# 512-token input products for six more state blocks of an S5 scan kernel, and layernorm deviations and means for four chunks at once

## The chip, the cores and the metric

One NeuronCore of a Trainium2 chip. The metric is the device time of one execution in microseconds (us); the kernel before takes 250.15 us, median of 3 runs (250.13 to 250.19).

## The reference

Input A_x is 2048 tokens by 1024 columns in bf16. It is normalised per token (xn), and the output is x plus two branches of xn, cut here to what matters:

```python
xn = layernorm(x)
# branch A: a diagonal complex state space with P = 1024 states
Bu = einsum("bld,pd->blp", xn, B_bar)           # input products, complex
h[t] = Lam_bar * h[t-1] + Bu[t]                 # scan over 2048 tokens
y  = 2 * real(einsum("blp,dp->bld", h, C)) + xn * Dskip
# branch B: the two tokens with the largest xn @ w_r go through a gated MLP (F = 3584)
out = x + y + xn + scatter(mlp(xn[top2]))
```

## The kernel before, in words

**Tiles.** Tokens come in 16 chunks of 128 (c), 8 frames of 256 (f) and 4 super-frames of 512 (s). States come in 8 blocks of 128 (j), each with a real and an imaginary part (ri).

**Order of the work.** The body registers small tasks with a planner (`add`), each with an engine, a function and its dependencies. The long string `ORDER` lists all tasks in one fixed sequence, and `emit` issues them in it. So each engine's own queue is the subsequence of its tasks, and an engine that reaches a task whose input is not there waits, with all that stands behind it. A ring (`pl.ring`) bounds how many buffers a kind of tile has; the products' PSUM tiles `pB` have 3.

**A chunk's normalisation.** Chunks 0 to 5 get their mean and variance on VectorE (`bs.c`, `bn.c`, lines 312 to 320), the others on ScalarE (`sum.c`, `sq.c`). `rstd.c` (line 336, `inv_sqrt` at 281) is three ScalarE instructions on one column: logarithm `lv`, reciprocal deviation, and deviation (line 286). `nmr1.c` adds 1 to the deviation (GpSimd line 360, ScalarE line 369) and `mean.c` negates the negated mean (GpSimd line 363). `apply.c` writes the normalised chunk. For chunks 0 to 3 TensorE transposes it (`Tpe.c`, line 386) and `xnT.c` copies it out of PSUM (VectorE for chunk 0, ScalarE line 393 for the rest); later chunks are transposed by DMA (`T.c`).

**The start on TensorE.** 15 warming tasks (`warm`), the transposes of the first blocks of B (`tB.0`, `tB.1`, line 262; ScalarE copies them out as `B.0.0`, `B.0.1`), of the parameters (`pP`, line 474; VectorE `pcol`), and of the chunks. The transposed blocks `B.j.ri` for j over 0 come by DMA from SyncE's queue.

**Input products.** For the first two super-frames (s below `SFW = 2`) a task `Bu.f.j` (line 661) makes both parts of one block for a frame: 16 matmuls over 256 tokens, into one PSUM bank, which ScalarE copies out in one instruction (`u.f.j`, line 667). For f below 2 and j below 2 each is split in halves of 128 tokens (`Bh.f.j.ri`, then `Bu`). For the last two super-frames a task `Bs.s.j.ri` (line 672) makes one part for 512 tokens: 8 matmuls over 512 tokens, also one bank, and ScalarE copies it out in two instructions of 256 (`us.s.j.ri`, line 680).

**Scan and output.** Per frame VectorE turns the products (`TI.f`, lines 738 to 747), scans per chunk (`SC.c`, line 766); ScalarE casts (`gb.c`, line 772); GpSimd carries the state on (`cw.c` 782, `cy.c` 790, `cin.c` 797 and 798); VectorE turns back (`TO.c`, lines 808 to 817). Per chunk and column half (dh) ScalarE seeds a PSUM tile with xn (`seed.c.dh`, line 871), VectorE applies the skip row and the deviation (`sk.c.dh`, line 881), TensorE adds 16 matmuls of 512 columns (`Y.c.0` to `Y.c.3`, eight each, line 891; 0 and 1 are the left half, 2 and 3 the right), ScalarE adds the mean (`ADD.c.dh`, line 907), SyncE stores. These PSUM tiles are a ring of 3: `seed.2.0` takes the buffer that `ADD.0.1` gives back, which reads the end of `Y.0.3`.

Of the kernel before, what the change touches and what calls it, by code (L numbers as in the profile page):

```python
# [25 lines left out]
warm.0 warm.1 warm.2 warm.3 warm.4 warm.5 warm.6 Bn.0 x.0 xa bs.0 bn.0 rstd.0 pre x.1 bs.1 apply.0 bn.1 warm.7 warm.8 warm.9 warm.10 warm.11 warm.12  # L26
warm.13 warm.14 tB.0 start.0 nmean.1 x.2 B.1.0 x.3 Tpe.0 Bn.1 B.1.1 B.0.0 xnT.0 bs.2 rstd.1 apply.1 tB.1 Bh.0.0.0 Tpe.1 x.5 bn.2 bs.3 B.0.1 nmean.0
xnT.1 bn.3 rstd.2 B.2.0 Bh.0.0.1 pP.0 pcol.0 Bh.0.1.0 apply.2 rstd.3 dt frq x.4 B.3.0 B.2.1 Bu.0.0 u.0.0 Bh.0.1.1 Tpe.2 rad Bu.0.1 apply.3 xnT.2 Tpe.3
turns xnT.3 B.3.1 Bh.1.0.0 Bh.1.0.1 Bh.1.1.0 Bu.1.0 trig bs.5 B.4.0 u.0.1 whole angle bn.5 nmean.5 abs u.1.0 sin den bs.4 first Bh.1.1.1 Bu.1.1 u.1.1
cos Bu.0.2 B.4.1 sq1.0 u.0.2 Bu.1.2 Bu.0.3 nmean.2 sq1.1 bn.4 log inv.0 rc.0 u.1.2 rstd.5 kappa mean.0 Bu.1.3 Bu.1.4 nmean.3 nmr.1 R0.0 apply.5 B.5.0  # L30
B.5.1 x.6 tan.0 inv.1 u.0.3 rc.1 tan.1 cs ntan.0 Bu.0.4 u.1.3 rstd.4 u.1.4 Bu.1.5 TI.0.0 ntan.1 u.0.4 ts.1.1 ends cin.0.0 nmr.5 ts.1.0 nmean.4 nmr1.2
nmr.0 apply.4 u.1.5 B.6.0 B.6.1 ts.0.0 Bu.0.5 Bu.0.6 u.0.5 T.5 sum.6 nmean.6 Bu.1.6 B.7.0 B.7.1 Bu.0.7 nmr1.1 T.4 x.7 nmr.4 R0.1 R.1 ts.0.1 u.0.6 sq.6
rstd.6 nmr1.6 nmr.6 apply.6 u.1.6 Bu.1.7 R.0 SC.0.0.0 xr.0 xnT.4 SC.0.0.1 C.0.1 sum.7 E2c.1 nmean.7 xnT.5 u.0.7 u.1.7 x.8 T.6 E2c.0 Bu.2.0 Bu.2.1
Bu.2.2 x.9 gb.0.0.0 sq.7 u.2.0 nmr1.3 cw.0.0 nmr1.0 seed.0.0 TI.0.4 E2s.0 wr cy.0.0 cin.1.0 rstd.7 gb.0.0.1 nmr.7 u.2.1 Bu.2.3 xnT.6 Bu.2.4 nmr.2
cin.0.4 SC.0.4.0 cw.0.4 SC.0.4.1 cy.0.4 apply.7 u.2.2 sum.8 Drow T.7 gb.0.4.0 u.2.3 xr.1 u.2.4 gb.0.4.1 E2n.0 xnT.7 SC.1.0.0 cw.1.0 cin.1.4 SC.1.0.1
E2s.1 SC.1.4.0 Bu.2.5 Bu.2.6 Bu.2.7 u.2.5 nmean.8 E2n.1 SC.1.4.1 nmr1.4 u.2.6 sq.8 nmr.3 TO.0.4 C.0.0 sk.0.0 seed.0.1 sk.0.1 u.2.7 seed.1.0 sum.9
nmean.9 Bu.3.0 u.3.0 gb.1.0.0 rstd.8 gb.1.4.0 sq.9 TO.0.0 nmr.8 mean.2 gb.1.4.1 Bu.3.1 u.3.1 apply.8 gb.1.0.1 Bu.3.2 u.3.2 Bu.3.3 rstd.9 Y.0.0 Y.0.1
C.1.0 TI.1.0 u.3.3 ADD.0.0 nmr.9 apply.9 cw.1.4 cy.1.4 cin.2.4 cy.1.0 Bu.3.4 Bu.3.5 x.11 Bu.3.6 T.8 Y.0.2 TO.1.4 cin.2.0 SC.2.0.0 sk.1.0 x.10 E2t.1
TO.1.0 u.3.4 seed.1.1 sum.10 nmean.10 sq.10 C.1.1 cw.2.0 gb.2.0.0 SC.2.0.1 cy.2.0 cin.3.0 T.9 xr.2 x.12 Y.1.0 Y.0.3 sk.1.1 rstd.10 mean.1 E2t.0
gb.2.0.1 Y.1.1 Bu.3.7 SC.3.0.0 sum.11 nmean.11 sq.11 nmr.10 ADD.0.1 apply.10 seed.2.0 rstd.11 TO.2.0 ADD.1.0 nmr.11 u.3.5 Y.1.2 Y.1.3 seed.2.1 ADD.1.1  # L40
out.0.1 apply.11 sk.2.0 T.10 x.15 out.0.0 SC.3.0.1 cw.3.0 sk.2.1 Y.2.0 gb.3.0.0 Y.2.1 Y.2.2 xnT.9 u.3.6 TI.2.0 xr.3 gb.3.0.1 u.3.7 T.11 sum.15 sum.12
ADD.2.0 Y.2.3 mean.10 cy.3.0 cin.4.0 SC.4.0.0 cw.4.0 xnT.11 nmean.15 xnT.8 xnT.10 sq.15 TO.3.0 SC.4.0.1 cy.4.0 mean.3 mean.7 nmean.12 seed.3.0 sk.3.0
rstd.15 Bs.2.0.0 us.2.0.0 Bs.2.0.1 cin.5.0 out.2.0 Bs.2.1.0 Bs.2.1.1 seed.3.1 us.2.0.1 ADD.2.1 gb.4.0.0 us.2.1.0 gb.4.0.1 Bs.2.2.0 TO.4.0 SC.5.0.0
SC.5.0.1 Y.3.0 xr.5 xr.4 us.2.1.1 x.13 seed.4.0 x.14 sq.12 nmr.15 rstd.12 apply.15 us.2.2.0 nmr.12 apply.12 out.1.1 T.15 sk.3.1 Bs.2.2.1 Bs.2.3.0
us.2.2.1 us.2.3.0 Bs.2.3.1 Bs.2.4.0 Y.3.1 Y.3.2 gb.5.0.0 out.1.0 mean.5 mean.12 cw.5.0 gb.5.0.1 cy.5.0 cin.6.0 nmr1.5 nmr1.10 sum.13 nmean.13 us.2.3.1
TI.3.0 SC.6.0.0 T.12 mean.4 SC.6.0.1 cw.6.0 cy.6.0 mean.11 us.2.4.0 Bs.2.4.1 cin.7.0 sq.13 ADD.3.0 rstd.13 xnT.12 seed.4.1 us.2.4.1 sum.14 nmean.14
sq.14 nmr.13 sk.4.0 sk.4.1 rstd.14 nmr.14 Y.3.3 Bs.2.5.0 gb.6.0.0 us.2.5.0 apply.14 Bs.2.5.1 Bs.2.6.0 Y.4.0 Y.4.1 Bs.2.6.1 out.2.1 gb.6.0.1 T.14
apply.13 T.13 xnT.15 xnT.13 ADD.3.1 nmr1.9 us.2.5.1 TO.5.0 xnT.14 SC.7.0.0 Y.4.2 ADD.4.0 us.2.6.0 seed.5.0 us.2.6.1 TO.6.0 Y.4.3 r.0 seed.5.1 out.4.0
out.3.0 gb.7.0.0 Bs.2.7.0 Bs.2.7.1 sk.5.0 w.0 SC.7.0.1 cand ADD.4.1 sk.5.1 us.2.7.0 us.2.7.1 w.1 xr.6 out.3.1 w.2 w.3 TI.4.0 Y.5.0 Y.5.1 ADD.5.0
gb.7.0.1 idx cw.7.0 cy.7.0 cin.8.0 seed.6.0 gather SC.8.0.0 SC.8.0.1 Bs.3.0.0 Bs.3.0.1 seed.6.1 us.3.0.0 Y.5.2 us.3.0.1 sk.6.0 bns gb.8.0.1 nmr1.13  # L50
cw.8.0 cy.8.0 xz Bs.3.1.0 us.3.1.0 Bs.3.1.1 Bs.3.2.0 us.3.1.1 us.3.2.0 Y.5.3 ADD.5.1 rstds Y.6.0 Bs.3.2.1 gb.8.0.0 us.3.2.1 out.5.0 w.4 sig TO.7.0
norm Bs.3.3.0 w.5 cin.9.0 sT out.5.1 xT SC.9.0.0 gb.9.0.0 nmr1.15 Y.6.1 mm.0 SC.9.0.1 sk.6.1 cw.9.0 nmr1.8 nmr1.7 mean.6 cy.9.0 TI.5.0 xr.7 Bs.3.3.1
gb.9.0.1 us.3.3.0 us.3.3.1 seed.7.0 sk.7.0 out.4.1 cin.10.0 Bs.3.4.0 Y.6.2 Y.6.3 mean.13 w.6 sig1 TO.8.0 ADD.6.0 w.7 w.8 w.9 Y.7.0 w.10 w.11 ADD.6.1
seed.7.1 sk.7.1 SC.10.0.0 xr.8 Bs.3.4.1 Bs.3.5.0 mm.1 Y.7.1 Y.7.2 SC.10.0.1 cw.10.0 ymb0 us.3.4.0 cy.10.0 us.3.4.1 seed.8.0 xr.9 exp.0 ADD.7.0
gb.10.0.0 out.6.0 TO.9.0 out.6.1 Bs.3.5.1 gu.0 gb.10.0.1 sk.8.0 Y.7.3 us.3.5.0 seed.8.1 ADD.7.1 Bs.3.6.0 us.3.5.1 us.3.6.0 Bs.3.6.1 mean.8 cin.11.0
SC.11.0.0 SC.11.0.1 cw.11.0 cy.11.0 cin.12.0 mean.9 w.12 Bs.3.7.0 w.13 w.14 w.15 w.16 w.17 out.7.0 out.7.1 xr.10 gb.11.0.1 seed.9.0 gb.11.0.0 nmr1.11
Bs.3.7.1 us.3.6.1 us.3.7.0 us.3.7.1 sk.8.1 gT.0 mm.2 exp.1 TO.10.0 sk.9.0 Y.8.0 Y.8.1 Y.8.2 Y.8.3 ADD.8.0 w.18 w.19 w.20 w.21 w.22 w.23 w.24 w.25
out.8.0 seed.9.1 ADD.8.1 TI.6.0 SC.12.0.0 SC.12.0.1 Y.9.0 cw.12.0 seed.10.0 sk.9.1 TO.11.0 sk.10.0 Y.9.1 Y.9.2 gb.12.0.1 ADD.9.0 xr.11 out.9.0 out.8.1
seed.10.1 mm.3 Y.9.3 xr.12 gb.12.0.0 cy.12.0 cin.13.0 SC.13.0.0 nmr1.12 sk.10.1 Y.10.0 gu.1 Y.10.1 Y.10.2 Y.10.3 cw.13.0 mean.14 gb.13.0.0 ADD.9.1
TO.12.0 w.26 w.27 w.28 seed.11.0 exp.2 ADD.10.0 seed.11.1 gT.1 mm.4 sk.11.0 ADD.10.1 sk.11.1 SC.13.0.1 w.29 w.30 out.9.1 w.31 w.32 w.33 w.34 w.35  # L60
out.10.0 xr.13 out.10.1 seed.12.0 sk.12.0 gu.2 TI.7.0 gT.2 Y.11.0 Y.11.1 ADD.11.0 seed.12.1 Y.12.0 Y.12.1 Y.11.2 Y.11.3 xr.14 gb.13.0.1 TO.13.0
sk.12.1 cy.13.0 ADD.11.1 ADD.12.0 exp.3 cin.14.0 SC.14.0.0 cw.14.0 seed.13.0 seed.13.1 sk.13.0 SC.14.0.1 mm.5 Y.12.2 Y.12.3 cy.14.0 cin.15.0 out.11.1
gb.14.0.0 gu.3 sk.13.1 ADD.12.1 gb.14.0.1 Y.13.0 Y.13.1 Y.13.2 Y.13.3 out.11.0 w.36 w.37 w.38 out.12.0 TO.14.0 w.39 nmr1.14 seed.14.0 ADD.13.0
ADD.13.1 sk.14.0 SC.15.0.0 hot w.40 seed.14.1 out.13.0 w.41 out.12.1 gT.3 xr.15 Y.14.0 Y.14.1 SC.15.4.0 SC.15.0.1 sk.14.1 SC.15.4.1 mm.6 Y.14.2
ADD.14.0 seed.15.0 seed.15.1 SC.15.6.0 rows Y.14.3 ADD.14.1 seed.15.2 TO.15.0 sk.15.1 sk.15.0 TO.15.4 row_.3 out.13.1 row_.2 out.14.0 SC.15.6.1
# [1133 lines left out]
```

## Time and profile before

| | |
|---|---|
| median of 3 runs | 250.15 us (250.13 to 250.19) |
| the profiled execution | 250.2 us, of it 248.1 us in the profile's span and 2.1 us around it |
| TensorE | 241.1 us busy |
| VectorE / ScalarE / GpSimd | 231.0 / 177.4 / 92.1 us busy |
| TensorE's granted clock | 0.998 of full |

The profile lists instructions by engine: PE is TensorE, PEld its weight loads, DVE VectorE, ACT ScalarE, POOL GpSimd, SPq SyncE's DMA issues. The chain of waits follows the execution back from its last instruction: each piece is what released the next. A group "x48" is that many instructions of one line. Matmuls overlap in their pipeline, so the length of one in a list is more than the step from one to the next; steps are read from groups.

### The profile page before, as it was taken

How to read it: one execution, taken by the hardware profiler on the slowest of the kernel's cores; microseconds unless marked ns; L12 is line 12 of the kernel's file. 1: busy time of each engine (PE TensorE's matmuls, PEld its weight loads, DVE VectorE, ACT ScalarE, POOL GpSimd, SP SyncE). 2: the span in 40 equal slices, each digit the busy share in tenths (PEclk: the TensorE clock that was granted, in tenths of full speed). 3: DMA queues.
4: the chain of work that ended last, by engine and by line, in shares of the span. 5: the costliest groups of instructions: out<-in, count | busy, mean ns of one | idle time of the engine just before them, and what ended most of it. 6: DMA issues, size and time to landing. Idle time of an engine off the chain costs nothing.

```text
span 248.1 us, 4602 instructions
## 1 busy us (share of the span) xinstructions
PE 241.1 (97%) x1723; PEld 139.9 (56%) x1743; DVE 231.0 (93%) x267; ACT 177.4 (71%) x364; POOL 92.1 (37%) x148
## 2 busy tenths in 40 slices
...
GB/s 206 237 190 150 210 171 249 144 274 131 237 144 109 106 97 114 127 3 10 118 184 248 165 0 116 393 225 320 274 176 400 251 376 340 281 202 391 66 64 44
DMA packets 66753, 46.77 MB, mean 189 GB/s; under 512 B 46114, under 2 KB 52648, under 8 KB 66732
## 3 DMA queue, kind: packets, MB, share of 16 engines
...
q8 instruction: 13, 0.21, 0.3%
q10 hardware_dynamic: 192, 0.07, 0.1%
q14 instruction: 8, 0.07, 0.1%
...
## 4 chain that ended last, share of the span: by engine, by line
PE 94%; DMA 2%; issue 1%; DVE 1%; SPq 1%
PE pY L891 44%; PE pB L661 23%; PE pB L672 22%; PE pG L1086 3%; DMA xt<-in_A_x_dram 2%; PE pD L1117 1%; PE r_ps L404 1%; DVE ot L905 1%; PE pT L386 1%; SPq L180 0%; SPq L168 0%; DVE xn L346 0%; SPq L169 0%; PE pY L896 0%; PE pP L474 0%
## 5 line engine op out<-in xcount | busy, mean ns | idle before, releaser
L891 PE MATMUL pY<-CT,hT 128*128 128x512 bf16 (+1 forms) x515 | 113.1, 372 | 0.9 <-issue 0.3
L891 PEld LDWEIGHTS <-hT 128*128 128x128 bf16 x528 | 51.2, 98 | 58.9 <-issue 1.9
L766 DVE TENSOR_TENSOR_SCAN gf<-R,v 128x1040 f32<-128x1040 f32 (+1 forms) x34 | 68.9, 2055 | 1.4 <-POOL v L798 1.0
L782 POOL TENSOR_TENSOR cw<-gf,tL 128x16 f32<-128x16 f32 (+1 forms) x34 | 33.4, 984 | 97.5 <-DVE gf L766 89.8
L672 PE MATMUL pB<-xnT,BT 128*128 128x512 bf16 x249 | 57.0, 379 | 0.4
L661 PE MATMUL pB<-xnT,BT 128*128 128x256 bf16 (+1 forms) x576 | 57.3, 261 | 0.0
L661 PEld LDWEIGHTS <-BT 128*128 128x128 bf16 x576 | 51.1, 98 | 5.6
L907 ACT ACTIVATE ot<-pY,mean_all 128x512 bf16<-128x512 f32 x30 | 20.5, 686 | 33.4 <-PE pY L891 33.2
L672 PEld LDWEIGHTS <-BT 128*128 128x128 bf16 x256 | 24.8, 98 | 30.4 <-PE pG L1086 0.4
L772 ACT CAST gb<-gf 128x1024 bf16<-128x1024 f32 (+1 forms) x34 | 31.8, 940 | 7.5 <-DVE gf L766 7.3
L808 DVE TENSOR_TENSOR m<-gb,E 128x4096 bf16<-128x4096 bf16 x13 | 29.5, 2271 | 0.5 <-ACT gb L772 0.5
L680 ACT CAST u<-pB 128x256 bf16<-128x256 f32 x64 | 19.9, 376 | 10.0 <-PE pB L672 8.0
L871 ACT ACTIVATE pY<-xr,nmr_all,rstd_all 128x512 f32<-128x512 bf16 (+1 forms) x33 | 25.2, 770 | 0.3
L881 DVE SCALAR_TENSOR_TENSOR pY<-Drow,std_all,pY 128x512 f32<-128x512 bf16 (+1 forms) x33 | 23.5, 723 | 0.6 <-ACT pY L871 0.6
L667 ACT CAST u<-pB 128x512 bf16<-128x512 f32 x32 | 18.2, 578 | 2.1 <-PE pB L661 2.0
L810 DVE TENSOR_TENSOR hT<-m 128x2048 bf16<-128x2048 bf16 x13 | 15.9, 1225 | 1.2
L740 DVE TENSOR_TENSOR v<-u,m 128x4096 bf16<-128x4096 bf16 x7 | 16.0, 2292 | 0.2
L738 DVE TENSOR_TENSOR m<-u,E1t 128x4096 bf16<-128x4096 bf16 x7 | 16.0, 2283 | 0.0
L798 POOL TENSOR_TENSOR v<-cy,v 128x16 bf16<-128x16 f32 (+1 forms) x17 | 14.2, 837 | 1.4
L350 ACT ACTIVATE xn<-xt,nmr_all,rstd_all 128x1024 bf16<-128x1024 bf16 x10 | 12.4, 1238 | 0.1
L332 ACT ACTIVATE xn<-xt,nmean_all 128x1024 bf16<-128x1024 bf16 x10 | 11.5, 1153 | 0.1
L797 POOL CAST v<-cy 128x16 bf16<-128x16 f32 (+1 forms) x17 | 10.4, 610 | 0.8
...
## 6 DMA issues: line engine op xcount, KB each, us to landing
...
wt<-in_B_w_down_dram SPq DMA_DIRECT2D x4, 1024.0 KB, 10.7
...
```

Source lines behind the costliest of these rows:

```text
L661: nc.tensor.matmul(out=pB[:, ri, ts_], lhsT=BT[ri][j][:, k, :], rhs=xnT_frame(f)[:, k, ts_], start=(k == 0), stop=(k == DT - 1))
L667: nc.scalar.copy(out=u_tiles[f][:, :, :, j, :].rearrange("p c i t -> p i c t"), in_=pB_tiles.pop((f, j))[:].rearrange("p i (c t) -> p i c ...
L672: nc.tensor.matmul(out=pB[:], lhsT=BT[ri][j][:, k, :], rhs=xnT_tiles[s][:, k, :], start=(k == 0), stop=(k == DT - 1))
L680: nc.scalar.copy(out=u_tiles[f][:, :, ri, j, :], in_=pB[:, i * TF:(i + 1) * TF].rearrange("p (c t) -> p c t", c=CPF))
L766: nc.vector.tensor_tensor_scan(out=flat(gf), data0=flat(R[:, js, :]), data1=flat(v[:, ri, js, :]), initial=0.0, op0=ALU.mult, op1=ALU.add)
L772: nc.scalar.copy(out=gb_tiles[c][:, ri, js, :], in_=gf_tiles[c, js.start, ri][:, :, 2:])
L782: nc.gpsimd.tensor_tensor(out=cw_tiles[c, js.start][:, ri, :, 0:n], in0=g.unsqueeze(1).to_broadcast([128, 2, n]), in1=tL[:, ri, :, js], op ...
L808: nc.vector.tensor_tensor(out=m[:].rearrange("p k i j t -> p k (i j t)"), in1=E2[:].rearrange("p k i j t -> p k (i j t)"), in0=flat(gb[:]) ...
L871: nc.scalar.activation(out=pY[:, 0:d_.stop - d_.start], in_=y_tiles["xr", c][:, d_], func=ACT.Identity, bias=nmr_all[:, c:c + 1], scale=rs ...
L881: nc.vector.scalar_tensor_tensor(out=pY, in0=ms["Drow"][:, d_], scalar=std1_all[:, c:c + 1], in1=pY, op0=ALU.add, op1=ALU.mult)
L891: nc.tensor.matmul(out=pY, lhsT=h_tiles[c][:, ri, j, :], rhs=CT[ri][h][:, j, d0:d0 + w], start=False, stop=end, skip_group_check=True)
L907: nc.scalar.activation(out=ot, in_=pY, func=ACT.Identity, bias=mean_all[:, c:c + 1])
```

## The change

What it does, part by part.

1. `HY = (3, 7, 0, 0)` replaces `SFW`: in super-frame 0 the blocks 3 to 7, in super-frame 1 block 7, are made by `Bs` tasks of 512 tokens. That is six blocks; 192 matmuls of 256 tokens become 96 of 512, and 12 copies `u` become 24 narrower ones.
2. The logarithms of all chunks are kept (`lv_all`). `rstd.c` is two instructions. The deviations of four chunks are made by one instruction (`std.g`), the 1 is added for four by one GpSimd instruction (`nmr1.g`), and `mean.g` does four means. Each waits for all four chunks.
3. `ORDER` is written anew throughout.

```diff
-    SFW = 2
+    HY = (3, 7, 0, 0)
...
+    lv_all = consts.tile([128, NCH], F32, name="lv_all")
...
     def ln_rstd(c, scale):
-        inv_sqrt(rstd_all[:, c:c + 1], ln_part[c][:, 1:2], 128, scale, std1_all[:, c:c + 1])
+        nc.scalar.activation(out=lv_all[:, c:c + 1], in_=ln_part[c][:, 1:2], func=ACT.Ln, bias=eps_t[:], scale=scale)
+        nc.scalar.activation(out=rstd_all[:, c:c + 1], in_=lv_all[:, c:c + 1], func=ACT.Exp, scale=-0.5)
+
+    def ln_std(g):
+        nc.scalar.activation(out=std1_all[:, 4 * g:4 * g + 4], in_=lv_all[:, 4 * g:4 * g + 4], func=ACT.Exp, scale=0.5)
...
-    def ln_std1(c):
-        nc.gpsimd.tensor_scalar_add(out=std1_all[:, c:c + 1], in0=std1_all[:, c:c + 1], scalar1=1.0)
-
-    def ln_mean(c):
-        nc.gpsimd.tensor_scalar_mul(out=mean_all[:, c:c + 1], in0=nmean_all[:, c:c + 1], scalar1=-1.0)
+    def ln_std1(g):
+        nc.gpsimd.tensor_scalar_add(out=std1_all[:, 4 * g:4 * g + 4], in0=std1_all[:, 4 * g:4 * g + 4], scalar1=1.0)
+
+    def ln_mean(g):
+        nc.gpsimd.tensor_scalar_mul(out=mean_all[:, 4 * g:4 * g + 4], in0=nmean_all[:, 4 * g:4 * g + 4], scalar1=-1.0)
...
-    def ln_std1_act(c):
-        nc.scalar.activation(out=std1_all[:, c:c + 1], in_=std1_all[:, c:c + 1], func=ACT.Identity, bias=one_t[:])
...
+    for g in range(NSF):
+        four = range(4 * g, 4 * g + 4)
+        add(("std", g), "ACT", 0.2, lambda g=g: ln_std(g), [("rstd", c) for c in four] + [("log",)], key=4 * g - 24)
+        add(("nmr1", g), "POOL", 0.3, lambda g=g: ln_std1(g), [("std", g)], key=4 * g - 24)
+        add(("mean", g), "POOL", 0.3, lambda g=g: ln_mean(g), [("nmean", c) for c in four], key=4 * g - 24)
...
-    for s in range(SFW, NSF):
-        for j in range(PT):
+    for s in range(NSF):
+        for j in range(HY[s], PT):
             for ri in range(2):
...
-    for f in range(2 * SFW):
-        for j in range(PT):
+    for f in range(NF):
+        for j in range(HY[f // 2]):
```

The new `ORDER`, as the queues that it gives to the engines at the places that matter here ("..." is the same or without interest):

```
TensorE, start, before: warm x15  tB.0 Tpe.0 tB.1 Bh.0.0.0 Tpe.1 Bh.0.0.1 pP Bh.0.1.0 Bu.0.0 Bh.0.1.1 Tpe.2 Bu.0.1 Tpe.3
                        Bh.1.0.0 Bh.1.0.1 Bh.1.1.0 Bu.1.0 Bh.1.1.1 Bu.1.1 Bu.0.2 Bu.1.2 ...
TensorE, start, after:  warm x15  Tpe.0 tB.0 tB.1 pP Tpe.1 Bh.0.0.0 Bh.0.1.0 Bh.0.0.1 Tpe.2 Bu.0.0 Bh.1.0.0 Bh.1.0.1
                        Bh.1.1.0 Bh.0.1.1 Tpe.3 Bu.0.1 Bh.1.1.1 Bu.1.0 Bu.1.1 Bu.0.2 Bu.1.2 Bs.0.3.0 ... Bs.0.7.1 Bu.2.0 ...
VectorE, start, before: ... bs.2 apply.1 bn.2 bs.3 bn.3 pcol apply.2 frq apply.3 turns ...
VectorE, start, after:  ... bs.2 apply.1 bn.2 apply.2 pcol bs.3 frq bn.3 turns apply.3 ...
ScalarE, start, before: rstd.0 B.0.0 rstd.1 B.0.1 xnT.1 rstd.2 rstd.3 dt u.0.0 rad xnT.2 xnT.3 ...
ScalarE, start, after:  rstd.0 rstd.1 B.0.0 B.0.1 rstd.2 xnT.1 dt xnT.2 u.0.0 rstd.3 rad trig xnT.3 ...
TensorE, later, before: Bu.3.6 Y.0.2 Y.1.0 Y.0.3 Y.1.1 Bu.3.7 Y.1.2 Y.1.3 Y.2.0 Y.2.1 Y.2.2 Y.2.3 Bs.2.0.0 ...
TensorE, later, after:  Bu.3.6 Bs.1.7.0 Y.0.2 Bs.1.7.1 Y.1.0 Y.0.3 Y.1.1 Y.1.2 Y.2.0 Y.2.1 Y.2.2 Y.2.3 Y.1.3 Bs.2.0.0 ...
ScalarE, later, before: ... ADD.0.1 apply.10 seed.2.0 rstd.11 ADD.1.0 ...
ScalarE, later, after:  ... apply.10 sq.11 ADD.0.1 us.1.7.0 seed.2.0 ADD.1.0 sum.12 seed.2.1 us.1.7.1 ...
GpSimd, later, after:   ... cw.2.0 mean.0 nmr.3 mean.1 cy.2.0 ...
SyncE, start, before:   x.2 B.1.0 x.3 B.1.1 x.5 B.2.0 x.4 B.3.0 B.2.1 B.3.1 B.4.0 B.4.1 B.5.0 B.5.1 x.6 B.6.0 B.6.1 T.5 B.7.0 B.7.1 T.4 ...
SyncE, start, after:    x.2 B.1.0 x.3 B.1.1 x.4 B.2.0 B.2.1 B.3.0 x.5 B.4.0 B.3.1 B.5.0 B.4.1 x.6 B.5.1 T.4 B.6.0 B.6.1 B.7.0 B.7.1 x.7 T.5 ...
```

## Rows read from the trace of the kernel before

**Rows 1.** The page's first part: busy time, share of the span and instructions.
```profile
PE 241.1 (97%) x1723; PEld 139.9 (56%) x1743; DVE 231.0 (93%) x267; ACT 177.4 (71%) x364; POOL 92.1 (37%) x148
```

**Rows 2.** All waits of TensorE: who waited for whom, total us, times, longest.
```profile
PE warm L409 <- POOL ident masks.py:199: 1.4, 1, 1.4
PE pT L386 <- DVE xn L346: 0.9, 1, 0.9
PE pT L262 <- DMA Bn<-in_A_B_im_dram: 0.3, 1, 0.3
PE pY L891 <- issue: 0.3, 2, 0.2
```

**Rows 3.** Pieces of the chain that ended last: start us, us, what.
```profile
8.70 0.62 PE pT L386 x8
...
9.77 0.12 PE pP L474
...
12.37 0.89 PE pB L661 x16
13.26 0.45 PE pT L386 x8
13.71 45.49 PE pB L661 x448
...
62.65 5.24 PE pB L661 x48
...
76.55 0.65 PE pY L891 x3
...
138.95 5.18 PE pB L672 x24
...
243.96 1.57 DVE ot L905 x3
```

**Rows 4.** The timeline of the start: start us, us, engine, line, instruction, count.
```profile
7.14 0.61 PE L661 MATMUL pB<-xnT,BT 128*128 128x128 bf16 x8
...
9.28 0.21 DVE L320 BATCH_NORM_AGGREGATE mv<-st 128x2 f32<-128x12 f32 x1
...
10.27 0.30 ACT L283 ACTIVATE lv<-mv,eps_t 128x1 f32<-128x1 f32 x1
...
10.85 0.54 DVE L346 TENSOR_SCALAR xn<-xt,mv,rstd_all 128x1024 bf16<-128x1024 bf16 x1
...
12.40 1.01 ACT L393 COPY xnT<-pT 128x1024 bf16<-128x1024 bf16 x1 [0.19 <-PE pT L386]
```

**Rows 5.** Groups by line and shape: count, busy us, mean ns of one, idle before.
```profile
L661 PEld LDWEIGHTS <-BT 128*128 128x128 bf16 x576 | 51.1, 98 | 5.6
...
L680 ACT CAST u<-pB 128x256 bf16<-128x256 f32 x64 | 19.9, 376 | 10.0 <-PE pB L672 8.0 <-remote 2.0
L667 ACT CAST u<-pB 128x512 bf16<-128x512 f32 x32 | 18.2, 578 | 2.1 <-PE pB L661 2.0
...
L286 ACT ACTIVATE std_all<-lv 128x1 f32<-128x1 f32 x16 | 3.0, 186 | 0.0
...
L369 ACT ACTIVATE std_all<-std_all,one_t 128x1 f32<-128x1 f32 x10 | 2.7, 289 | 0.0
```

**Rows 6.** One 5 us window: busy us (count) by engine, TensorE's clock, DMA.
```profile
45.00:50.00 5.00, 5.00 (x49) 4.47 (x47) 4.80 (x8) 5.00 (x10) 4.76 (x8) 1.00 0.46 111
```

**Rows 7.** The timeline of SyncE's queue: the last transposing load of B.
```profile
28.92 1.48 SPq L240 DMA_TRANSPOSE BT<-in_A_B_im_dram  x1
```

**Rows 8.** The page's DMA issues: count, median us from issue to landing.
```profile
BT<-in_A_B_im_dram SPq DMA_TRANSPOSE x7, 4.1
```

**Rows 9.** The timeline before Y.2.0: the add of (0,1), the seed, the skip.
```profile
75.05 0.67 ACT L907 ACTIVATE ot<-pY,mean_all 128x512 bf16<-128x512 f32 x1
76.75 0.76 ACT L871 ACTIVATE pY<-xr,nmr_all,rstd_all 128x512 f32<-128x512 bf16 x1
...
77.55 0.75 DVE L881 SCALAR_TENSOR_TENSOR pY<-Drow,std_all,pY 128x512 f32<-128x512 bf16 x1
```

More of the change, by code (lines that the diff above doesn't have):

```diff
@@ L25 @@
 ORDER = """
[L26 to L65, printed above, removed]
@@ L66 @@
-sk.15.2 out.14.1 row_.1 ymb TO.15.6 Y.15.0 Y.15.1 Y.15.2 Y.15.3 Y.15.4 Y.15.5 Y.15.6 hotY.15.0 hotY.15.1 ADD.15.0 fix Y.15.7 hotY.15.2 out.15.0 Y.15.8
-ADD.15.1 out.15.1 ADD.15.2 out.15.2
+xa bs.0 x.0 bn.0 rstd.0 Bn.0 x.1 bs.1 apply.0 bn.1 pre warm.0 warm.1 warm.2 warm.3 warm.4 warm.5 start.0 Bn.1 x.2 rstd.1 B.1.0 warm.6 warm.7 warm.8
+warm.9 warm.10 warm.11 warm.12 x.3 warm.13 warm.14 Tpe.0 tB.0 tB.1 xnT.0 B.0.0 bs.2 B.1.1 apply.1 pP.0 Tpe.1 bn.2 B.0.1 rstd.2 apply.2 pcol.0 Bh.0.0.0
+Bh.0.1.0 Bh.0.0.1 xnT.1 Tpe.2 dt bs.3 xnT.2 nmean.0 nmean.1 Bu.0.0 frq bn.3 x.4 B.2.0 B.2.1 Bh.1.0.0 Bh.1.0.1 u.0.0 rstd.3 rad turns Bh.1.1.0 Bh.0.1.1
```

82 lines of the change are left out of this document (61 added, 21 removed).

## The prediction

> **What bounds the kernel now.** I read the busy shares first, then TensorE's waits, then the chain, then single stretches. TensorE is busy for 97% of the span [rows 1], and all its waits come to 2.9 us [rows 2]; the three that name a releaser fall before its first input product. From 13.71 us on, the chain is one run of TensorE's matmuls up to the last adds at 243.96 [rows 3]. The reader is to see that nothing else is on that path: VectorE at 93% and ScalarE, full in the window from 45 to 50 [rows 6], run beside it and finish in time. TensorE's granted clock in that window is 1.00, the 2.4 GHz level, and the change leaves its stream as dense. So the time moves by what TensorE's own instructions cost, and by any wait that the new order puts in front of one of them.
>
> **Part 1, the width.** 48 matmuls over 256 tokens took 5.24 us, 0.1092 each; 24 over 512 took 5.18, 0.2158 each [rows 3]. Two narrow ones cost 0.2184, so a pair saves 0.0026, and 96 pairs save **0.25 us**. The weight loads that go (96 of 98 ns [rows 5]) give nothing more: a step of 109 ns already hides them.
>
> ScalarE's copies: a block took two of 578 ns and will take four of 376 [rows 5], 0.35 us more, over six blocks 2.1 us. The gathered deviations take away 12 of 16 of 186 ns and ten of 289 [rows 5], 5.1 us. ScalarE has 3 us less to do. On the path both count nothing, because TensorE waits for neither [rows 2]; the cover is the ring of three `pB` tiles, which lets a copy be about two products (3.5 us) late. GpSimd, at 37% [rows 1], loses 13 small instructions net, at nothing too; what it gains is a wait for four chunks, which comes up below.
>
> **Part 2, the start.** Here the order changes what TensorE has to fill a wait with. `Tpe.1` starts at 8.70 in the trace, after 0.9 us for `apply.1` [rows 2, 3]. That wait remains: VectorE still has `bs.2` ahead of `apply.1`, and SyncE's queue is the same up to `x.3`.
> Before, `Bh.0.0.0` ran inside the wait, at 7.14 [rows 4]. From the end of `Tpe.1`, 8.70 + 0.62 = 9.32, it took 4.39 to 13.71 [rows 3], with 4.13 of work in it (nine groups of eight narrow matmuls or transposes at 0.445, half of the 0.89 that 16 take, and `pP` at 0.12), then 64 more narrow ones at 0.89 per 16, 3.56. The set of the four halved products was done at 17.27.
> After, `pP` (0.12) is in the wait and `Bh.0.0.0` (0.45) behind it. Step by step:
> - Three `Bh` after 9.32: 3 x 0.445, to 10.66.
> - `Tpe.2` needs `apply.2`. `bn.2` ends at 9.28 + 0.21 = 9.49 and ScalarE is free by then. From `lv` to the start of `apply` were 0.58, which took 0.54 [rows 4]: `apply.2` ends near 10.65, `Tpe.2` starts at 10.70 and ends 0.62 later, at 11.32. Without a wait it had ended at 11.11: **0.21 lost**.
> - `Bu.0.0`, 0.89, to 12.21. `Bh.1.0.0` now stands right behind it and needs ScalarE's copy of chunk 2. That starts 0.03 after the transposes and takes 1.01 [rows 4]: 12.37, so the product ends at 12.42 + 0.61 = 13.03 instead of 12.66: **0.37 lost**.
> - The rest meets no wait by the same walk (`apply.3` ends near 13.98, `Tpe.3` has its turn at 14.2): five groups of eight and three of 16, 4.90, to 17.93.
>
> So TensorE is **0.66 us later** after the same work. Lower bound 0.1: neither wait comes, and only the swap of `Bh.0.0.0` and `pP` (0.33) stands against the 0.26 of stall that the old order had. Upper bound 1.0: the small exponent `dt` and `pcol` push the copy of chunk 2 back by as much as one more narrow product. I take the walk.
>
> Behind that SyncE's queue has `T.4` ahead of four loads of B. By VectorE's new queue `apply.4` is done before that turn comes, so it holds nothing up; if it were late, the loads behind it would be. The last load was issued at 28.92 [rows 7], landing 4.1 later [rows 8], and 512-token products reach block 7 only near 35 (17.93, two products of 1.75 and eight of 1.73); the loads of x that changed place are as early. Nothing, with over 1 us of cover.
>
> **Part 3, the middle.** `TI.0.4` and `TI.2` now wait for 512-token products, which end later; VectorE reaches them no earlier, so nothing. The place with the least room is `Y.2.0`. Before, the add of (0,1) came at 75.05, its seed at 76.75, the skip ended at 77.55 + 0.75 = 78.30 [rows 9]. `Y.1.2` started at 76.55 [rows 3], and with `Y.1.3` behind it (8 x 0.2158 = 1.73 each) `Y.2.0` started near 80.0: 1.7 us of room. The new order moves `Y.1.3` behind `Y.2.3`, which takes exactly that. TensorE's own delay (0.66 - 0.25) gives 0.41 back: `Y.1.2` starts near 76.96 and `Y.2.0` has its turn 1.73 later, near 78.7.
> Its skip cannot be much earlier. `Y.0.3` ends one group (`Y.1.1`) ahead of `Y.1.2`, near 75.2; then ScalarE does the add (0.67), two copies of `us.1.7.0` (2 x 0.3 as they overlap, from 0.376), the seed (0.76), and VectorE the skip (0.75): 77.9 if ScalarE is free at 75.2. It isn't quite: the squares of chunk 11 stand ahead, and further up `ADD.0.0` has come to wait for `mean.0`, which waits on GpSimd behind `cw.2.0`. I reckon ScalarE 0.5 to 1 us behind, so the wait is between 0 (ScalarE free) and 0.8 (1.6 us behind). I take **0.15**, nearer to the low end, since VectorE and ScalarE did meet their turns without a wait throughout the old trace [rows 2].
>
> **Part 4, the end.** The last matmuls and adds are the same in number, the patch for the two tokens is issued behind the same stores. VectorE's new queue has the last skip ahead of the turn that `Y.15.3` needs; by my walk that still ends 0.3 us before it is wanted, the next tightest place. Nothing.
>
> **Sum.** -0.25 + 0.66 + 0.15 = +0.56. The profiled execution took 250.2 (span 248.1 and 2.1 around it), which gives 250.76; it lies 0.05 above the median of the runs, so **250.7 us** against that. All bounds at their ends: -0.25 + 0.1 + 0 = -0.15, and -0.25 + 1.0 + 0.8 = +1.55. A measurement of this kernel can tell about 0.2%, 0.5 us, from no change: the line to slower is at 250.65, just under the forecast.
>
> **Rivals.**
> *The skip is in time, not slower by 0.2%.* Place: ScalarE between the end of `Y.0.3` and `seed.2.0`. If the square of chunk 11 is done when `Y.0.3` ends, the skip ends at 77.9, ahead of its turn, and 250.15 + 0.41 = 250.55 is left, within 0.2%. For it: ScalarE's 3 us less work. Against: it was full all through this stage [rows 6]. It decides at 0.8 us of lateness of ScalarE.
> *The start loses nothing.* ScalarE or VectorE are quicker than walked and TensorE finds chunk 2 there twice: 250.15 - 0.15 = 250.0. Against: both waits hang on durations that the rows give.
> *The weight loads come out too, faster.* If 256-token products were held up by their loads, each of the 96 that go would give up to its 98 ns, 9.4 us, and the time would be 240.7. Against: the steps of 0.1092 and 0.2158, which are the columns' time at 2.4 GHz (0.1067 and 0.2133) plus under 3 ns. The Trainium skill (TensorE: Matmul & The Clock Gate, Back-to-back issue gap) has a rule that points this way: a stream of load and matmul pairs should settle near 131 ns per 512 columns. By it 192 x 0.1092 - 96 x 0.131 = 8.4 us would be saved; the trace disagrees, at 215.8 ns in such a stream.
> *ScalarE falls behind for good.* In the second super-frame a copy that comes more than two products late holds `pB` and stops TensorE; each further us then costs one. Two of the copies that it would have to catch up with, 1.1 us, make 251.8. Against: no such wait in the old trace [rows 2].
>
> **How the numbers follow.** The forecast's case, between 250.65 and 251.3, has 0.45; the skip in time 0.35; the start without loss 0.08; ScalarE behind for good 0.07; weight loads 0.03; 0.02 is left for a gain that I haven't found. Slower by over 0.2% is the forecast and ScalarE behind, and a little from the edges: 0.53. Within 0.2% is the skip in time and most of the start without loss: 0.42. Faster: 0.05. The range runs from 250.0, the start without loss, to 251.5, the upper bounds short of their joint end; it leaves out the weight loads and most of ScalarE behind. The likeliest case's own range is 250.65 to 251.3.
>
> **What would show it.** Right: two waits of TensorE near 10.7 (for an `apply` on VectorE) and near 12.4 (for the copy of chunk 2), the first product of `Bu.0.2` or `Bu.1.2` near 17.9, the six blocks' 96 products at steps of 0.2158, and a short wait for VectorE's skip near 78.7. Wrong: no wait in the start and the dense run beginning at 17.3 or before; a step of a 512-token product that isn't 0.216; a wait of TensorE elsewhere above 0.5 us, above all for a copy `us` or `u` between 50 and 66.

## The result and the profile after

The changed kernel took **253.96 us** (median of 6 runs, 252.98 to 254.5), the kernel before 250.14 on the same chip: a ratio of 1.015, with a 95% interval of 1.0128 to 1.0171. The forecast was 250.7 with a range up to 251.5: the direction was right, the size was not, by 3.3 us. The profiled execution of after took 253.88, its span is 252.1.

The page's first part, as in [rows 1]:

```profile
PE 241.2 (96%) x1624; PEld 130.9 (52%) x1647; DVE 231.9 (92%) x267; ACT 175.8 (70%) x354; POOL 96.3 (38%) x135
```

TensorE's busy time is that of before (241.1), so its 3.8 us are not work. All waits of TensorE, as in [rows 2]:

```profile
PE warm L408 <- POOL ident masks.py:199: 1.4, 1, 1.4
PE pT L385 <- DVE xn L348: 1.3, 2, 0.8
PE pY L901 <- issue: 0.6, 4, 0.2
PE pY L901 <- DVE pY L891: 0.5, 1, 0.5
PE pB L662 <- ACT xnT L392: 0.2, 1, 0.2
```

Two kinds of wait are new: for the copy of chunk 2 (L392), as forecast, and for a skip (L891), but not the one forecast. They don't make 3.8 us either. The timeline of TensorE and of the final adds:

```profile
12.34 1.95 PE L662 MATMUL pB<-xnT,BT 128*128 128x128 bf16 x32 [0.21 <-ACT xnT L392]
...
182.65 1.89 PE L901 MATMUL pY<-CT,hT 128*128 128x512 bf16 x8 [0.51 <-DVE pY L891]
...
245.39 1.57 DVE L915 TENSOR_SCALAR ot<-pY,nmean_all 128x512 bf16<-128x512 f32 x3 [1.50 <-PE pY L901]
```

The last adds start at 245.39 instead of 243.96 [rows 3], so TensorE is only **1.43 us** late. The other 2.25 us of the 3.68 between the profiled times (253.88 against 250.2) come behind it; the spans differ by 4.0, and by them it is 2.6. SyncE's queue at the end says where, and the scatter-add that GpSimd issues behind it; columns are start, us, engine, line, instruction and count, first after, then before:

```profile
237.59 1.36 SPq L1142 DMA_DIRECT2D ymb<-ym  x2
239.06 0.35 SPq L921 DMA_DIRECT2D out_dram<-ot  x1
239.45 0.59 SPq L1142 DMA_DIRECT2D ymb<-ym  x1
240.08 9.65 SPq L921 DMA_DIRECT2D out_dram<-ot  x5
246.12 1.42 POOL L1146 DMA_INDIRECT out_dram<-ymb,idx_t  x1 [19.82 <-issue]
```

```profile
236.49 0.74 SPq L1132 DMA_DIRECT2D ymb<-ym  x1
237.28 0.35 SPq L911 DMA_DIRECT2D out_dram<-ot  x1
237.67 0.60 SPq L1132 DMA_DIRECT2D ymb<-ym  x1
238.32 0.87 SPq L911 DMA_DIRECT2D out_dram<-ot  x2
239.23 0.59 SPq L1132 DMA_DIRECT2D ymb<-ym  x1
244.91 0.97 SPq L911 DMA_DIRECT2D out_dram<-ot  x2
242.06 1.42 POOL L1136 DMA_INDIRECT out_dram<-ymb,idx_t  x1 [17.66 <-issue]
```

`fix`, GpSimd's scatter-add of the two patched rows, waits for the row transfers (`ymb<-ym`) and for every store of chunks 0 to 14; the stores of chunk 15 wait for `fix`. In the new order `out.13.0` and `out.13.1` stand behind the three row transfers, which wait for ScalarE until 237.59; before, `out.13.0` was ahead of them and `out.13.1` behind the first. The chain that ended last, in order of time, shows what that led to:

```profile
240.58 0.38 SPq L921
240.96 0.04 issue
241.00 3.85 DMA out_dram<-ot
244.85 0.03 issue
...
245.84 1.70 POOLq L1204
```

The last store takes 3.85 us to land, where the median of the run's stores is 3.1. `fix` is issued at 246.12 (242.06 before), and the stores of chunk 15 go out near 249 instead of 245, with their adds long done. What the store was doing is seen in the DMA view of two windows of after, 240 to 242.7 and 242.7 to 244.65:

```profile
q1 hardware_dynamic: 550, 0.50, 54.8%
q8 instruction: 1, 0.02, 3.4%
...
DMA packets 10, 0.02 MB, mean 8 GB/s; under 512 B 1, under 2 KB 9, under 8 KB 9
...
q1 hardware_dynamic: 9, 0.01, 2.5%
q14 instruction: 1, 0.01, 1.7%
```

From 242.7 on the DMA engines are all but idle, and still nine packets of the stores' queue (q1) are missing: 8 rows and a semaphore, a sixteenth of one store's 128 rows, which came at 243.70 to 244.39, while the others had ended at 242.47. What went ahead is the one packet of q8, the queue named instruction, 16,384 bytes, 242.25 to 243.71 in the trace's DMA records: the eight rows begin as it ends. (The packet of q14 in the second window starts behind them, at 244.58.) By the queue's name such packets bring an engine's program; in before there is none between 231.3 and the stores of chunk 15.

So there were three suspects: (A) the stores' place in SyncE's queue, (E) the instruction packet, (C) TensorE's own 1.43 us; and against all three, the parts of the change themselves.

### The profile page after: what moved, and what is told of

Its sections match the earlier page's. It is cut to its first block, busy times and chain, and to the rows that moved or that the text cites. A ratio compares the mean times of both kernels' runs of the same rounds, so it can differ in the third digit from the quotient of the medians.

```text
span 252.1 us, 4403 instructions
## 1 busy us (share of the span) xinstructions
PE 241.2 (96%) x1624; PEld 130.9 (52%) x1647; DVE 231.9 (92%) x267; ACT 175.8 (70%) x354; POOL 96.3 (38%) x135
## 5 line engine op out<-in xcount | busy, mean ns | idle before, releaser
L673 PE MATMUL pB<-xnT,BT 128*128 128x512 bf16 x341 | 78.0, 379 | 0.5
L792 POOL TENSOR_TENSOR cw<-gf,tL 128x16 f32<-128x16 f32 (+1 forms) x34 | 34.8, 1025 | 96.7 <-DVE gf L776 84.4
L673 PEld LDWEIGHTS <-BT 128*128 128x128 bf16 x352 | 34.4, 98 | 41.2 <-PE pG L1096 0.4
L681 ACT CAST u<-pB 128x256 bf16<-128x256 f32 x88 | 27.5, 374 | 16.3 <-PE pB L673 16.0
L662 PE MATMUL pB<-xnT,BT 128*128 128x256 bf16 (+1 forms) x384 | 36.2, 255 | 0.2 <-ACT xnT L392 0.2
L662 PEld LDWEIGHTS <-BT 128*128 128x128 bf16 x384 | 32.3, 98 | 3.8 <-issue 0.3
L891 DVE SCALAR_TENSOR_TENSOR pY<-Drow,std_all,pY 128x512 f32<-128x512 bf16 (+1 forms) x33 | 23.5, 725 | 2.2 <-ACT pY L881 2.1
L807 POOL CAST v<-cy 128x16 bf16<-128x16 f32 (+1 forms) x17 | 15.9, 938 | 0.8
L800 POOL TENSOR_TENSOR cy<-cw 128x16 f32<-128x16 f32 (+1 forms) x17 | 12.8, 754 | 1.3
L808 POOL TENSOR_TENSOR v<-cy,v 128x16 bf16<-128x16 f32 (+1 forms) x17 | 12.4, 728 | 1.4
```

The costliest lines, as they stand in the source:

```text
L662: nc.tensor.matmul(out=pB[:, ri, ts_], lhsT=BT[ri][j][:, k, :], rhs=xnT_frame(f)[:, k, ts_], start=(k == 0), stop=(k == DT - 1))
L673: nc.tensor.matmul(out=pB[:], lhsT=BT[ri][j][:, k, :], rhs=xnT_tiles[s][:, k, :], start=(k == 0), stop=(k == DT - 1))
L681: nc.scalar.copy(out=u_tiles[f][:, :, ri, j, :], in_=pB[:, i * TF:(i + 1) * TF].rearrange("p (c t) -> p c t", c=CPF))
L792: nc.gpsimd.tensor_tensor(out=cw_tiles[c, js.start][:, ri, :, 0:n], in0=g.unsqueeze(1).to_broadcast([128, 2, n]), in1=tL[:, ri, :, js], op ...
L891: nc.vector.scalar_tensor_tensor(out=pY, in0=ms["Drow"][:, d_], scalar=std1_all[:, c:c + 1], in1=pY, op0=ALU.add, op1=ALU.mult)
```

## The experiments

Times are medians; each ratio is against runs of the kernel before on the same chip (250.41 for e_stores, e_late, e_width and e_gather; 250.17 for e_skip, e_skip_head, e_tail and e_best; 250.38 for e_fetch, e_fetch_2 and e_head2; 250.35 for e_best2).

**e_stores: the stores of chunk 13 early again.** In the hand-written order of after:

```
-out.12.0 SC.15.0.0 ... row_.2 ymb out.13.0 Y.15.0 ... TO.15.6 out.13.1 Y.15.3
+out.12.0 out.13.0 out.13.1 SC.15.0.0 ... row_.2 ymb Y.15.0 ... TO.15.6 Y.15.3
```

> The kernel after, with the two stores of chunk 13 (`out.13.0`, `out.13.1`) put ahead of the row transfers on SyncE's queue, all else as it is. Theory A (late stores hold back the scatter-add): the last store of a chunk below 15 is issued near 239.9 instead of 240.96, lands near 243, the scatter-add lands near 246.8 instead of 248.85, and the run takes about 252.0 us, 1.2 to 2.4 less than the kernel after. Rival B (all that is lost is TensorE's, whose last instruction comes 1.4 us later than before): no change, 253.9.

252.3 us, 1.0094 (1.006 to 1.0128): 1.4 (by the ratios) to 1.7 less than after, as theory A had it. `fix` is issued at 243.30, and the instruction packet (242.18) comes after the last row of these stores (241.68). That cure takes away both A's cause and E's collision, so it doesn't tell them apart.

**e_late: the kernel before with after's queue.**

```
-out.13.0 w.41 ... row_.3 out.13.1 row_.2 out.14.0 SC.15.6.1 sk.15.2 out.14.1 row_.1
+w.41 ... row_.3 row_.1 out.14.0 row_.2 out.13.0 out.14.1 out.13.1 SC.15.6.1 sk.15.2
```

> The kernel before, with SyncE's queue at the end in the order of the kernel after: `row_.3`, `row_.1`, `out.14.0`, `row_.2`, `out.13.0`, `out.14.1`, `out.13.1`. Nothing of the change is in it. Theory A: the last store lands near 243.5, the scatter-add near 247.4 instead of 244.9, and the run takes 252.1 to 252.7 us, 2.0 to 2.6 more than the kernel before, with TensorE's end unmoved. Rival B: 250.1, as before.

251.37 us, 1.0041 (1.0018 to 1.0063): slower, by 1.0 and not by 2.0 to 2.6. (The 1.0 is read from the medians; in the trace TensorE also starts 0.66 us late, for a load of B.) The same stores, in the same order and issued 0.45 us earlier than in after, land by 242.0 here:

```profile
239.63 7.71 SPq L911 DMA_DIRECT2D out_dram<-ot  x5
...
243.65 1.42 POOL L1136 DMA_INDIRECT out_dram<-ymb,idx_t  x1 [18.59 <-issue]
```

So the late queue is a cost by itself, but not the whole one. What e_late lacks is the instruction packet, of which it has none between 232.0 and 248.6: it has the TensorE program of before.

**e_fetch and e_fetch_2: the packet moved.** Small matmuls at the end of the warm-up, where TensorE has nothing to do, push the boundary at which the next stretch of its program is fetched.

```
+    def keep_clock_pads():
+        keep_clock()
+        for _ in range(24):
+            nc.tensor.matmul(out=warm[0:2, 0, 0:32], lhsT=ident[:, 0:2], rhs=ident[:, 0:32], start=True, stop=True)
```

> The kernel after, with 24 more small matmuls (2 columns of weights, 32 columns wide) at the end of the warm-up, where TensorE waited 0.5 to 1.2 us for the first normalised chunk. In the trace of after a transfer of 16,384 bytes on the queue named instruction stands at 242.38 to 243.85, and the last 8 rows of a store in front of the scatter-add end at 244.52 instead of 242.6; such transfers come once per some 256 instructions of TensorE. Theory E (the instruction transfer holds up the store): 48 more instructions move it 5.2 us earlier, to about 237.2, ahead of the stores; the scatter-add is issued 1.5 to 1.9 us earlier, the run takes 252.0 to 252.5 us, with TensorE's end unmoved and SyncE's queue as in after. Rival F (the five stores late on SyncE's queue land slowly by themselves): no change, 253.9.

> The kernel after with 2 such small matmuls more instead of 24. Theory E: the instruction transfer moves by 0.4 us only, to about 242.0, and still meets the last stores: 253.3 to 254.2 us. Rival G (more warm-up work by itself helps): as e_fetch.

e_fetch took **251.93** us, 1.0057 (1.004 to 1.0075), e_fetch_2 **253.41**, 1.0115 (1.0084 to 1.0147). The two differ in 22 small matmuls. In e_fetch the packet stands at 236.31 and the DMA engines are empty where they crept before. (The expectation for e_fetch counts the packet and the rows from a start 0.13 us earlier than the span's; here all times count from the span's.) The DMA view of e_fetch from 243.3 to 244.7 and its scatter-add, then those of e_fetch_2, from 243 to 244.7:

```profile
DMA packets 0, 0.00 MB, mean 0 GB/s; under 512 B 0, under 2 KB 0, under 8 KB 0
...
244.55 1.41 POOL L1151 DMA_INDIRECT out_dram<-ymb,idx_t  x1 [18.03 <-issue]
```

```profile
DMA packets 9, 0.01 MB, mean 5 GB/s; under 512 B 1, under 2 KB 9, under 8 KB 9
...
246.21 1.42 POOL L1151 DMA_INDIRECT out_dram<-ymb,idx_t  x1 [19.69 <-issue]
```

The same nine packets, late again, in e_fetch_2, where the instruction packet lies at 242.28 to 243.80 and the eight rows begin at 243.78. `fix` is issued at 244.55 in e_fetch and at 246.21 in e_fetch_2, while the last adds start together (245.62 and 245.60). Theory E is shown: the collision costs about **1.5 us** (0.6 to 2.4 by the two intervals; the two traces differ by 1.66). That 48 more TensorE instructions move the packet by 5.9 us also shows whose program it is, and so does a count: in all fourteen traces the last packet of 16,384 bytes is the thirteenth, and when it starts TensorE has started 3,227 to 3,261 matmuls and loads of those recorded. The Trainium skill (Runtime: NRT & Kernel Launch, Instruction fetch mechanics) says the program is fetched in blocks of 16 KiB, 256 instructions, on a DMA queue of the engine's own, and that a crossing is mostly hidden. The traces agree: 16,384 bytes each, and 13 packets for 3,314 matmuls and loads in e_stores; hidden it is from TensorE, whose step stays at 0.216 there, but not from the store behind it.

**e_width and e_gather: each part alone, in the order of before.**

```
-Bu.0.3 ... Bu.1.3 Bu.1.4 ... Bu.0.4
+Bs.0.3.0 ... Bs.0.3.1 Bs.0.4.0 ... Bs.0.4.1
...
-    SFW = 2
+    HY = (3, 8, 0, 0)
```

> The kernel before with part 1 alone: five of eight state blocks of the first 512 tokens over 512 tokens, in the places where the pairs over 256 stood; order, statistics and the next 512 tokens as before. By the step durations read before (0.2158 against two of 0.1092), 80 pairs save 0.21 us: 249.9, if no copy of ScalarE comes late. Rival: four copies of 376 ns for two of 578 on a ScalarE that is full in this stretch make TensorE wait for a product's tile: up to five blocks of 0.35 us late, 250.3 to 251.9.

> The kernel before with part 2 alone: deviations and means for four chunks at once, put where the last of the four single ones stood ahead of the first skip; order otherwise as before. Theory: ScalarE has 5.1 us less to do, none of it on the path: 250.1, within 0.2%. Rival: with ScalarE relieved, VectorE's skips and copies start earlier and a wait of TensorE's goes: faster by more than 0.5 us. Rival on the other side: a skip waits for the statistics of four chunks, 0.2 to 0.8 slower.

e_gather keeps `SFW = 2`: 250.44, 0.9998 (0.9977 to 1.0018), no difference, and its waits are those of other runs in the order of before. e_width: 250.68, 1.0009 (0.9992 to 1.0026). The same stretch of products in the chain of e_gather, then of e_width:

```profile
86.92 8.63 PE pB L673 x40
```

```profile
86.70 8.63 PE pB L672 x40
```

TensorE is 0.22 us earlier, against 0.21 for the width, and the adds at the end start at 243.75 instead of 243.96. But the run is no shorter: with 160 instructions fewer the packet comes at 237.65 to 239.19, ahead of the last 8 rows of a store (239.18 to 239.87, the others ended at 238.44), SyncE's next store takes 1.44 us to issue instead of 0.39, and `fix` is issued at 242.90 instead of 242.06. It is the same collision, in its small form, by the change's own first part. That it ate the gain is read from this one trace; the medians alone would allow either.

**e_skip: two steps of VectorE moved**, on top of e_stores.

```
-cin.11.0 SC.11.0.0 TO.10.0 SC.11.0.1 sk.8.1 ... gu.0 sk.8.0
+cin.11.0 sk.8.0 SC.11.0.0 TO.10.0 SC.11.0.1 sk.8.1 ... gu.0
...
-ADD.12.0 hot sk.13.0 ... sk.14.1 out.12.0
+ADD.12.0 sk.13.0 ... sk.14.1 hot out.12.0
```

> The kernel after with the stores of chunk 13 early (as in e_stores) and two steps of VectorE's order moved: `sk.8.0` to before `SC.11.0.0`, where VectorE waited 0.78 us for GpSimd, and `hot` to after `sk.14.1`. Theory C (the rest of the loss is TensorE's, by waits for late skips and head): the waits ahead of Y.8.0 (0.67 us between matmuls beyond the usual pitch) and Y.14.0 (0.31) go, and the run takes 251.3 us, 1.0 less than e_stores. Rival D (TensorE's waits are covered by the scatter-add): 252.3 as e_stores.

250.91 us, 1.0028 (1.0008 to 1.0048): 1.4 less by the medians, 1.65 by the ratios. Both waits are gone, and the last adds start at 244.09, 1.47 earlier than in e_stores (245.56), which had also waited 0.37 for `Y.7`. TensorE's list of e_skip has no skip in it:

```profile
PE pT L385 <- DVE xn L348: 2.0, 2, 1.2
PE warm L408 <- POOL ident masks.py:199: 1.4, 1, 1.4
PE pY L901 <- issue: 0.6, 4, 0.2
PE pB L662 <- ACT xnT L392: 0.2, 1, 0.2
```

Theory C holds, for the two skips: 0.67 + 0.31 = 0.98. The other part of the 1.47 is not of this edit: `Tpe.1` came 0.13 earlier, and the wait ahead of `Y.7`, which stands before both moved steps, differs from trace to trace (0.11 in after, 0.40 in e_fetch_2, none in e_fetch). About 0.5 of what is left lies behind the adds: the last 8 rows of the last store end at 247.41 while its others end at 246.89, behind a packet of another instruction queue (q14, 246.60 to 246.91) and nine packets of ScalarE's store (246.91 to 247.13).

**e_skip_head and e_head2: the start.** The first takes the order of before up to `Bu.1.2`; the second keeps the new start, gives TensorE other work in its two waits, and puts the three row transfers side by side:

```
-Bh.0.0.1 xnT.1 Tpe.2 dt ... xnT.2 ... Bu.0.0 ... Bh.1.0.0 Bh.1.0.1 u.0.0 rstd.3 ... Bh.1.1.0 Bh.0.1.1 apply.3 Tpe.3 trig Bu.0.1
+Bh.0.0.1 xnT.1 Bh.0.1.1 Bu.0.0 dt ... rstd.3 Tpe.2 u.0.0 xnT.2 ... apply.3 Bu.0.1 Tpe.3 Bh.1.0.0 Bh.1.0.1 Bh.1.1.0 trig
```

> e_skip with the first steps, up to `Bu.1.2`, in the order of the kernel before. Theory C: TensorE reaches the first product over 512 tokens 0.58 us earlier, and the run takes 250.7 us, within 0.2% of the kernel before: then start, two late skips and the stores are the whole of the loss. Rival D: 251.5 or more, something of the change itself, as the gathered statistics or the width, costs time in the middle.

> e_skip (stores of chunk 13 early, `sk.8.0` and `hot` moved) with the start mended: `Bh.0.1.1` and `Bu.0.0` ahead of `Tpe.2`, `rstd.3` ahead of `u.0.0` and of the copy `xnT.2`, and `Bh.1.0.0` to `Bh.1.1.0` behind `Tpe.3`, so that TensorE has work of the first two chunks while it waits for `apply.2` and the copy; and the three row transfers side by side. From `Tpe.1` to the first product over 512 tokens the kernel after takes 12.56 us, the order of before 11.91 (e_width, e_best). Theory: 12.0, the run is 0.5 us shorter than e_skip, 250.3 or less, and not slower than before. Rival: `apply.3` comes too late for `Tpe.3` and nothing is gained, 250.9.

Both missed: 251.26, 1.0041 (1.0023 to 1.006), and 251.59, 1.0054 (1.0035 to 1.0073), neither better than e_skip. With the old start `Tpe.1` came at 8.97 (8.42 in e_skip): TensorE waited 0.9 us for the two halves of B, which it transposes behind the first chunk in the new start; SyncE loads both in the same order in before and after. From `Tpe.1` on it took 11.91 us again, but a wait of 0.4 for a copy followed. In e_head2 the two waits only moved:

```profile
13.74 0.62 PE L385 MATMUL pT<-ident,xn 128*128 128x128 bf16 x8 [0.53 <-DVE xn L348]
14.20 1.95 PE L662 MATMUL pB<-xnT,BT 128*128 128x128 bf16 x32
16.57 5.44 PE L662 MATMUL pB<-xnT,BT 128*128 128x128 bf16 x64 [0.42 <-ACT xnT L392]
```

`Tpe.3` and the copy of chunk 3 are now late, and the first product over 512 tokens starts at 21.85 instead of 20.98. I read from this that the start is set by the statistics of the four chunks, one behind another, and that filling one hole opened the next; no run shows it by itself.

**e_tail, e_best, e_best2: a version that beats both?** e_tail reorders SyncE's end of before; e_best adds the width of the first 512 tokens and the gathered statistics; e_best2 takes the first steps from after.

```
-row_.3 out.13.1 row_.2 out.14.0 SC.15.6.1 sk.15.2 out.14.1 row_.1
+out.13.1 out.14.0 row_.3 row_.2 row_.1 out.14.1 SC.15.6.1 sk.15.2
```

> The kernel before with another order on SyncE's queue at the end: `out.13.1`, `out.14.0`, `row_.3`, `row_.2`, `row_.1`, `out.14.1`. If the scatter-add and TensorE end close together there, as in e_late and e_width: the scatter-add is issued 0.3 to 0.8 us earlier, the run gains 0 to 0.4, 250.2. If TensorE alone sets the end: 250.4, no change.

> The order of the kernel before, with part 1 for the first 512 tokens, part 2, and the queue of e_tail at the end. With the scatter-add out of the way the 0.21 us of the width count, 250.0 us, faster than both. If the scatter-add still sets the end: 250.4.

> e_best with the first steps, up to `apply.1`, in the order of the kernel after: the first chunk and its statistics ahead of the first block of B, `rstd.1` ahead of ScalarE's copy of that block; from there the order of before, which takes 11.91 us from `Tpe.1` to the first product over 512 tokens. In the traces `Tpe.1` starts at 8.42 to 8.63 with the start of after (after, e_stores, e_skip) and at 8.69 to 9.36 with that of before. Theory: `Tpe.1` at 8.5, the first product over 512 tokens at 20.4, 249.8 us, 0.1 to 0.4 less than before. Rival: `Bh.0.0.0` then waits for ScalarE's copy and pushes `Tpe.1` back: 250.2, as before.

e_tail: 250.12, 0.9995 (0.998 to 1.001), though `fix` is issued at 241.61 instead of 242.06: in before TensorE sets the end and the scatter-add is just hidden. e_best: 250.05, 0.9999 (0.9982 to 1.0017). e_best2: **249.95, 0.9982 (0.9972 to 0.9993)**, the only one of the twelve experiments that beats both kernels, the one before by 0.2 to 0.7 us; an interval of 95% can miss once in twelve tries, so this is a hint. Its reason is not the one expected: in its trace `Bh.0.0.0` waits and `Tpe.1` comes at 9.16, as the rival said. The profiled run is the longest of its eleven (250.32), so the trace may not show what the median gained, and the cause stays open:

```profile
8.70 0.62 PE L662 MATMUL pB<-xnT,BT 128*128 128x128 bf16 x8 [0.66 <-ACT BT L265]
9.16 0.61 PE L385 MATMUL pT<-ident,xn 128*128 128x128 bf16 x8
```

## Why the prediction was wrong, point by point

**The view of the bound** was half right. TensorE does set the end of before (e_tail), but "nothing else is on that path" hid that the scatter-add ended at its heels: e_late added 1.0 us without a change to TensorE's program. The chain of waits shows one path; what runs second, by how little, it doesn't show. And not all three waits "fall before its first input product": the one for `apply.1` ends at 8.70, behind `Bh.0.0.0` at 7.14 [rows 4], as Part 2 of the prediction has it.

**Part 1, the width**, was right: 0.22 on TensorE against a term worked out as 0.21 for e_width's 80 pairs. The rival of the weight loads is out, with the Trainium skill's 131 ns (TensorE: Matmul & The Clock Gate, Back-to-back issue gap) that stood beside it: the steps stayed at 0.216. ScalarE's copies `u` and `us` made no wait in after and e_width, so ScalarE falling behind for good is out too, and e_gather shows the statistics at nothing beyond 0.2%.

**Part 2, the start**, was right in its mechanism and its size. Both waits came where the walk had them: ahead of `Tpe.2` (10.62) and ahead of `Bh.1.0.0` (12.34) TensorE's matmuls start 0.25 and 0.43 us after the one before, where this shape follows at 0.056 (0.89 for 16 [rows 3]), so 0.20 and 0.37 against 0.21 and 0.37. From `Tpe.1` to the first product over 512 tokens the new order takes 12.56 us (after, e_stores, e_skip), the old one 11.91 (e_width, e_best): 0.65 against a term of 0.66. "That wait remains" holds too, at 0.82 us; `Tpe.1` came 0.07 earlier than in before (8.63 against 8.70). At 87 us, where the third super-frame's products start, start and width together left TensorE 0.35 late; the terms made 0.41. TensorE in before, then in after:

```profile
86.74 8.80 PE L672 MATMUL pB<-xnT,BT 128*128 128x512 bf16 x39
```

```profile
87.09 12.03 PE L673 MATMUL pB<-xnT,BT 128*128 128x512 bf16 x54
```

**Part 3, the middle**, named the wrong skip. `Y.2.0` had no wait (0.15 forecast), as the first rival had it. The mechanism named, a skip that VectorE reaches late, came at `Y.8.0`: start to start 0.89 us instead of 0.22 between two matmuls, so 0.67; at `Y.14.0` 0.52, so 0.31; and 0.11 ahead of `Y.7`, for VectorE too. These 1.09 with the 0.35 make 1.44, all of TensorE's 1.43. The walk stopped at the first tight place. Why VectorE was late is seen in the timelines of VectorE and GpSimd in after:

```profile
168.06 2.27 DVE L818 TENSOR_TENSOR m<-gb,E 128x4096 bf16<-128x4096 bf16 x1
170.43 1.23 DVE L820 TENSOR_TENSOR hT<-m 128x2048 bf16<-128x2048 bf16 x1
172.44 2.33 DVE L776 TENSOR_TENSOR_SCAN gf<-R,v 128x1040 f32<-128x1040 f32 x1 [0.78 <-POOL v L808]
```

```profile
166.01 4.40 POOL L792 TENSOR_TENSOR cw<-gf,tL 128x16 f32<-128x16 f32 x2 [3.04 <-DVE gf L776]
170.49 1.25 POOL L800 TENSOR_TENSOR cy<-cw 128x16 f32<-128x16 f32 x1
...
180.59 0.23 POOL L792 TENSOR_TENSOR cw<-gf,tL 128x16 f32<-128x16 f32 x1 [3.56 <-DVE gf L776]
```

The scan of chunk 11 waited 0.78 for GpSimd, with four tasks of VectorE between it and `sk.8.0`; e_skip puts the skip into that hole, and the wait ahead of `Y.8.0` goes.

**Part 4, the end**, is the step that failed most: "the patch for the two tokens is issued behind the same stores. ... Nothing." They are the same stores, but the queue that issues them has another order, and I compared the engines' last steps without walking SyncE's. It cost 2.25 us behind the adds: about 1.5 of it the instruction packet (e_fetch against e_fetch_2), the rest the queue. Its price alone is 1.0 in the kernel before (e_late) and 0.7 here: e_fetch, with the late queue and without the collision, ends 4.80 us behind the start of its last adds (span 250.42, adds 245.62), before 4.13. A wait of that size at the end had no term and no rival. Rows for it were there: the issue of the last stores, of `fix`, and of the first store behind it.

**Of the sum**, 3.68 us between the two profiled runs: TensorE's 1.43, of it 0.35 the start less the width and 1.09 VectorE's late steps, and 2.25 behind it, about 1.5 the instruction packet and the rest the queue. The cures don't add up to this, as TensorE and the scatter-add run side by side: e_stores takes 1.4 to 1.7 away from after and e_fetch 2.0 to 2.3, by different cures of one delay. And e_stores and e_skip pay about 0.5 us that after does not: their last stores meet the packet of q14, which in after (250.92) comes behind the last row (250.74).
